# V of group 0 kept on chip, and w_down read in four chunks instead of two

## The chip, the cores and the metric

The kernel runs on one core of one Trainium2 chip. The metric is the device time of one execution in microseconds; less is better. A run is repeated and the median is given.

## The reference

One decode step (one token) of a transformer block, forward and backward, in bf16. With D = 448, 16 query heads, 8 groups of K and V, head size 256, a cache of 32,768 positions of which the last W = 4,096 are attended to, and a gated layer of width F = 1,792:

```python
h  = x + attention(layernorm(x), k_cache, v_cache, wq, wo)   # window: last 4096 positions
h2 = h + (layernorm(h) @ w_gate * (layernorm(h) @ w_up)) @ w_down
# outputs: h2, and the gradients of h2 for grad_out with respect to
# x, k_cache, v_cache, wq, wo, w_gate, w_up, w_down
```

The gradients of the two caches have the caches' full shape, 8 x 32,768 x 256 each. Outside the window they are zero, and these zeros have to be written: 28,672 positions of 256 elements for each group and cache. They are 235 MB of the 281 MB that the kernel writes.

## The kernel before

One large tile, `BIG`, holds nearly all of the on-chip data, by hand-made offsets. It is cut into slots of 8,192 elements a partition (16 KB); a slot takes the window of K or V of one group (partition p holds positions 32p to 32p + 31, as 32 rows of 256). A tile `zeros` has zeros in partitions 32 to 95, the source of the zero fill.

Transfers go out on two queues. SP (`FILL`) reads w_q and then writes zeros in 18 long transfers, one behind the other, over the whole run. GpSimd (`IO`) issues everything else: the loads of K, V and the weights in a fixed order (`io_load` orders each behind the one before it), the computed outputs, and the rest of the zero fill. That rest is dealt by `deal(eng, e0, k, n)`, which writes k x n rows of 16 KB from k source partitions, beginning at partition 32 + 4 e0; `deal_rest(0)` has four such transfers, behind the last load of w_down, and `deal_rest(1)` three, behind the last output.

Forward, for each group in turn (`moments`, `scores`, `softmax`): transposes of K on PE, scores, softmax, and the products of V with p and with p times K. K alternates between two slots (7 and 8). V of groups 0 to 6 was read into `V0` (rows 0 to 24 of group 0, a place of its own), slot 0 (rows 25 to 31 of group 0) and slots 1 to 6; V of group 7 then overwrites slot 0. So all of V but 7 rows of each partition of group 0 is still there for the backward stage.

Then w_o, w_gate and w_up are loaded over the K slots and the space behind them. w_down has 14 rows a partition, in two halves s of 7; one half fits into `wd_sb`. `down_grad(s)` (line 509) forms with DVE the gradient of the hidden values, one instruction of 448 elements for each row, and PE adds the half's share of the output `y` (line 535). The second half is loaded over the first, so its load waits for both. After the second half come the layernorm gradients, the gradients for gate and up (line 563), w_o (line 580) and wq.

Backward through attention, a step for each group in the order `SEQ` (1 to 7, then 0): `dP` transposes V of the next group and multiplies it by the output gradient, beside the 32 matmuls of the step (line 728), whose results go into a pair of slots (`PAIR`), from which two outputs of 2 MB, the window's part of the gradients of K and V, are written (line 737). A pair of slots may be written again when its earlier outputs have landed. `side` lists jobs behind each step: the outer products that form the weights' gradients, in halves of free slots, and the part that reads w_q again for the gradient of x. After step 5 the seven rows of V of group 0 are read once more (line 144), for the last step.

Of the kernel before, what the change touches and what calls it, by code (L numbers as in the profile page):

```python
# [7 lines left out]
bf16 = mybir.dt.bfloat16  # L8
f32 = mybir.dt.float32
# [5 lines left out]
D = 448  # L15
NI = 7
H = 16
G = 8
Dh = 256
W = 4096  # L20
T = 32
F = 1792
FC = 14
Sk = 32768
# [8 lines left out]

KS = 7
TAIL = 9 * SLOT
V0 = TAIL + 8256
NV0 = 25
SIZE = V0 + NV0 * Dh
RING = V0
K_SLOT = [KS + g % 2 for g in range(G)]  # L40
V_SLOT = [0, 1, 2, 3, 4, 5, 6, 0]


@with_exitstack
def kernel(
# [10 lines left out]

    BIG = const.tile([128, SIZE], bf16)
    x_bf = BIG[0:1, TAIL:TAIL + D]
    S_.dma_start(out=x_bf, in_=A_x.rearrange("a b d -> (a b) d"))
    go_bf = BIG[0:1, TAIL + 512:TAIL + 512 + D]  # L60
    S_.dma_start(out=go_bf, in_=grad_out.rearrange("a b d -> (a b) d"))
# [38 lines left out]
    def deal_rest(lap):  # L100
        if lap == 0:
            deal(IO, 0, 4, 25)
            deal(IO, 4, 3, 7)
            deal(IO, 7, 2, 15)
            deal(IO, 9, 7, 15)
        else:
            deal(IO, 0, 5, 2, 512)
            deal(IO, 5, 3, 25)
            deal(IO, 8, 8, 15)
            assert used[0] == 896 * ZW  # L110
# [10 lines left out]
    def slot(k):  # L121
        return BIG[:, k * SLOT:(k + 1) * SLOT]

    def half(k, h):
        return BIG[:, (2 * k + h) * SLOT // 2:(2 * k + h + 1) * SLOT // 2]

    def slot_kv(k):
        return slot(k).rearrange("p (t d) -> p t d", d=Dh)

    Kw = [slot_kv(k) for k in K_SLOT]  # L130
    Vw = [slot_kv(k) for k in V_SLOT]
    v0_head = BIG[:, V0:SIZE].rearrange("p (t d) -> p t d", d=Dh)

# [3 lines left out]
    def v_at(g, t):  # L137
        return v0_head[:, t, :] if g == 0 and t < NV0 else Vw[g][:, t, :]

    queued = [None]  # L140

    def io_load(out, in_):
        if queued[0] is None:
            queued[0] = IO.dma_start(out=out, in_=in_)
        else:
            with tc.issue_after(queued[0].ins):
                queued[0] = IO.dma_start(out=out, in_=in_)

    def load_window(dst, cache, g, n=1):
        src = cache[0, g, Sk - W:, :].rearrange("(p t) d -> p t d", t=T)  # L150
        for h in range(n):
            t = slice(h * T // n, (h + 1) * T // n)
            io_load(dst[:, t, :], src[:, t, :])
# [3 lines left out]

    def load_V(g, head=True):
        if g:
            load_window(Vw[g], A_v_cache, g)  # L160
            return
        src = A_v_cache[0, 0, Sk - W:, :].rearrange("(p t) d -> p t d", t=T)
        if head:
            io_load(v0_head, src[:, 0:NV0, :])
        io_load(Vw[0][:, NV0:T, :], src[:, NV0:T, :])

# [11 lines left out]
    make_identity(nc, ident_f[:])  # L178
    ones_bf = const.tile([1, 128], bf16)
    V_.memset(ones_bf[:], 1.0)  # L180
    ones_f = const.tile([128, 128], f32)
# [146 lines left out]
    def ring(k):  # L328
        return BIG[:, RING - (k + 1) * 1024:RING - k * 1024]

# [101 lines left out]
    WD0 = WG0 + NI * HF  # L432
    assert WD0 + FC // 2 * D == V0

# [11 lines left out]
    wu_sb = BIG[:, WU0:WO1]  # L446
    wd_sb = BIG[:, WD0:V0].rearrange("p (m n) -> p m n", n=D)
    bc2 = [BIG[:, o:o + F].rearrange("p (i c) -> p i c", i=2) for o in (WD0, WD0 - F)]
# [4 lines left out]
    for g in range(G):  # L453
        moments(g)
        if g + 2 < G:
            load_K(g + 2, 2)
        if g + 3 < G:
            load_V(g + 3)
        if g == G - 2:
            load_wo(0, 18)  # L460
        if g == 0:

            t = ps.tile([128, D], f32, tag="tmp", bufs=1)
            P_.matmul(t[:], lhsT=ones_bf[0:1, :], rhs=go_bf, start=True, stop=True)
            S_.copy(out=dh2_bc[:], in_=t[:])
# [31 lines left out]
    io_load(wu_sb, flat_rows(B_w_up))  # L497
    io_load(wd_sb, wd_rows[:, 0])
    hX = const.tile([128, NI], f32)
# [4 lines left out]
    for w, w_sb in ((0, wg_sb), (1, wu_sb)):  # L504
        wv = w_sb.rearrange("p (i c) -> p i c", i=NI)
        for m in range(NI):
            for i in range(NI):
                P_.matmul(gu_ps[:, w, :, m], lhsT=wv[:, i, m::NI], rhs=xx2[:, i, :], start=(i == 0), stop=(i == NI - 1))
    def down_grad(s):
        for m in range(NI):  # L510
            c = NI * s + m
            V_.tensor_tensor_reduce(out=dh_bc[:], in0=wd_sb[:, m, :], in1=dh2_bc[:], scale=1.0, scalar=0.0,
                                    op0=ALU.mult, op1=ALU.add, accum_out=d_hh[:, c:c + 1])

    down_grad(0)
    gu = const.tile([128, 2, FC], f32)
# [9 lines left out]
    V_.tensor_scalar(out=hX2[:], in0=hX[:], scalar1=0.5, scalar2=None, op0=ALU.mult)  # L526
    for s in range(2):
        if s:
            io_load(wd_sb, wd_rows[:, s])
            with tc.issue_after(queued[0].ins):  # L530
                deal_rest(0)
            down_grad(s)
        for m in range(NI):
            c = NI * s + m
            P_.matmul(y[:], lhsT=hh_bf[:, c:c + 1], rhs=wd_sb[:, m, :], start=(c == 0), stop=False, skip_group_check=True)
    half_to_row(y[:], hX2[:], False, first=False)
# [39 lines left out]
    for a in range(4):  # L576
        S_.copy(out=Mq[32 * a:32 * a + 32], in_=quarter(a))
    doW = small.tile([128, 32], f32, tag="doW", bufs=1)
    for b in range(32):
# [5 lines left out]
    V_.tensor_copy(out=doT[:], in_=doT_f[:])  # L585
    od = small.tile([128, 32], f32, tag="od", bufs=1)
    V_.tensor_tensor(out=od[:], in0=doT_f[:], in1=oT_f[:], op=ALU.mult)
# [3 lines left out]
    V_.tensor_copy(out=delta[:], in_=total(pd[:], H)[:])  # L591
    q_rows = BIG[0:H, TAIL:TAIL + Dh]
    do_rows = BIG[0:H, V0 - 320:V0 - 320 + Dh]
    rows16(qT, q_rows, SCALE)
# [3 lines left out]
    for h in range(H):  # L598
        for dk in range(2):
            for hf in range(2):  # L600
# [4 lines left out]
                          start=(hf == 0), stop=(hf == 1))  # L605
    kd = small.tile([128, H, 2], f32, tag="kd", bufs=1)
    V_.tensor_tensor(out=kd[:], in0=kbar[:].rearrange("p (h f) -> p h f", f=2), in1=delta[:].unsqueeze(2).to_broadcast([128, H, 2]), op=ALU.mult)
    dqd = small.tile([128, 32], f32, tag="dqd", bufs=1)
    V_.tensor_tensor(out=dqd[:], in0=dq_ps[:], in1=kd[:].rearrange("p h f -> p (h f)"), op=ALU.subtract)
# [26 lines left out]
    Pq = const.tile([128, NI], f32)  # L636
    wq2 = [slot(4)[:, (i % 4) * HQ:(i % 4 + 1) * HQ] for i in range(NI)]
    wq_d = flat_rows(A_wq).rearrange("p (i c) -> p i c", i=NI)

    def dxn_load(i0, i1):  # L640
        IO.dma_start(out=slot(4)[:, 0:(i1 - i0) * HQ].rearrange("p (i c) -> p i c", c=HQ), in_=wq_d[:, i0:i1, :])

# [5 lines left out]
    def dx_out():  # L648
        dxZ = layernorm_bwd(Pq[:], xh1[:], rstd1[:, 0:1], dhZ[:], 1.0, "dxZ")
        t = ps.tile([1, D], f32, tag="tmp", bufs=1)  # L650
        half_to_row(t[:], dxZ[:], False)
        dx = slot(4)[0:1, SLOT - D:SLOT]
        V_.tensor_copy(out=dx, in_=t[:])
        IO.dma_start(out=out_1.rearrange("a b d -> (a b) d"), in_=dx)
# [4 lines left out]
    def o5_job(buf, b):  # L659
        return lambda: outer(buf, o5[:, b:b + 8, :], b, b + 8, lambda n: dh_bc[:], oW, D)  # L660

    def o67_job(buf, w, i0, i1):
        return lambda: outer(buf, (o6, o7)[w][:, i0:i1, :], i0, i1, lambda i: bc2[w][:, i % 2, :], xf2, HF)

    def o8_job(buf, b):
        return lambda: outer(buf, o8[b // 7], b, b + 7, lambda n: dh2_bc[:], hh, D)

    SEQ = [1, 2, 3, 4, 5, 6, 7, 0]
    PAIR = [KS, 1, KS, 1, KS, 5, 1, KS]
    side = {  # L670
        0: [],
        1: [o67_job(half(3, 0), 0, 0, 4), o67_job(half(3, 1), 0, 4, 7)],
        2: [lambda: dxn_load(0, 4), o5_job(half(3, 0), 0), o5_job(half(3, 1), 8)],
        3: [lambda: dxn_part(0, 4), lambda: dxn_load(4, 7), o5_job(half(3, 0), 16)],
        4: [lambda: dxn_part(4, 7), dx_out, o5_job(half(3, 1), 24), o8_job(half(4, 0), 0)],
        5: [o8_job(half(4, 1), 7), o4_job(half(3, 0), 0), o4_job(half(3, 1), 2)],
        6: [o4_job(half(4, 0), 4), o4_job(half(0, 0), 6)],
        7: [],
    }
    o67_job(half(8, 1), 1, 0, 4)()  # L680
    o67_job(half(7, 1), 1, 4, 7)()


    bps = ctx.enter_context(tc.tile_pool(name="bps", bufs=1, space=bass.MemoryType.PSUM))
    vt_ctr = [0]
    Rb = BIG[:, TAIL + 256:TAIL + 1280].rearrange("p (k c) -> p k c", k=2)
    rows = BIG[:, TAIL + 1280:TAIL + 2304].rearrange("p (a c) -> p a c", a=8)
    VTb = [BIG[:, o:o + 1024] for o in (TAIL + 2304, WD0 + F)]

# [17 lines left out]
    for s, g in enumerate(SEQ):  # L707
# [17 lines left out]
        for t in range(T):  # L725
# [5 lines left out]
            if t % 4 == 3 and s + 1 < G:  # L731
                with tc.issue_after(mm.ins):
                    dP(s + 1, t // 4)
        if s == 5:
            load_V(0, False)
        for w, o in ((0, out_3), (1, out_2)):
# [36 lines left out]
```

## Time and profile before

| | |
|---|---|
| median of 3 runs | 782.29 us (781.71 to 782.57) |
| the profiled execution | 781.56 us; its span 779.8 us |
| moved | 331.13 MB: 49.84 MB read, 280.59 MB written (HBM) |
| mean rate | 425 GB/s |
| busy share of the span | PE 60%, DVE 51%, ACT 24%, POOL 5% |

The profile comes from one execution. "Busy tenths" cut the span into 40 equal slices and give the busy share of each in tenths. DMA is the mean over the core's 16 DMA engines; q1 is SP's queue and q0 is GpSimd's. The packets' own records (start, length, size and queue of each, without the engine's number) are used where a number for one packet is given. The landing time of a transfer goes from its issue to its completion. Line numbers are those of the kernel before.

### The profile page before, as it was taken

The page shows a single profiled execution, that of the slowest core. Times are in us where ns is not written, and L with a number is a line of the kernel's source. Part 1 is how long each engine was busy: PE and PEld are TensorE (multiplying, and loading weights), DVE is VectorE, ACT ScalarE, POOL GpSimd, SP SyncE. Part 2 cuts the span into 40 slices and gives each one's busy share as a digit, 9 for nine tenths or more (in the row PEclk, how much of TensorE's full clock was granted, in tenths as well). Part 3 has the DMA queues.
Part 4 walks back from the last instruction along what each step waited for, and adds up shares of the span by engine and source line. Part 5 has one row for each costly group of instructions (what it writes and reads, how often), then busy time and mean ns, then how long its engine had stood idle before and what let it go on. Part 6 is the DMA issues. An engine that isn't in the chain of part 4 may idle for free.

```text
span 779.8 us, 10845 instructions
## 1 busy us (share of the span) xinstructions
PE 470.1 (60%) x4374; PEld 263.1 (34%) x4419; DVE 401.4 (51%) x1169; ACT 188.7 (24%) x277; POOL 42.0 (5%) x86
## 2 busy tenths in 40 slices
PE   4798898899998642230579879382947696300000
PEld 3654554555564331030254334131423242000000
DVE  5377677677768222659335565367676554300000
ACT  0312322321120000351235435141514353200000
POOL 3000000000000001000000010101001100100000
PEclk9999989989999755555555555555555555555555
DMA  9999999999999999999999999999999999999998
GB/s 351 428 427 428 428 426 430 424 428 429 424 429 427 429 432 429 429 430 429 429 429 430 429 430 429 430 429 430 427 429 432 427 424 431 427 431 430 429 431 344
DMA packets 25234, 331.13 MB, mean 425 GB/s; under 512 B 2669, under 2 KB 2671, under 8 KB 4596
## 3 DMA queue, kind: packets, MB, share of 16 engines
q1 hardware_dynamic: 14557, 231.15, 69.5%
q0 software_dynamic: 10624, 99.29, 30.2%
q8 instruction: 34, 0.56, 0.3%
q14 instruction: 15, 0.12, 0.0%
q10 hardware_dynamic: 4, 0.00, 0.0%
HBM read 49.84 MB, written 280.59 MB: 424 GB/s over the span
## 4 chain that ended last, share of the span: by engine, by line
PE 41%; DMA 18%; DVE 12%; issue 12%; ACT 2%; POOL 1%; POOLq 0%; DVEq 0%; ACTq 0%
PE MT L402 14%; PE d_ps L728 7%; PE tr L345 7%; DMA out_dram<-BIG 6%; DMA BIG<-in_B_w_down_dram 5%; DMA BIG<-in_A_v_cache_dram 4%; DVE BIG L580 2%; PE sT L350 2%; DMA BIG<-in_A_k_cache_dram 2%; PE acc L405 1%; DVE BIG L563 1%; PE acc L408 1%; DMA BIG<-in_A_wq_dram 1%; DVE zeros L419 1%; ACT BIG L293 1%
## 5 line engine op out<-in xcount | busy, mean ns | idle before, releaser
L402 PE MATMUL MT<-BIG 128*128 128x512 bf16 x467 | 139.9, 408 | 1.9 <-DVE BIG L398 0.2
L398 DVE TENSOR_SCALAR BIG<-BIG,pf 128x256 bf16<-128x256 bf16 x512 | 114.3, 281 | 26.6 <-PE MT L402 23.6
L728 PE MATMUL d_ps<-BIG 32*128 32x512 bf16 x256 | 118.9, 620 | 9.1 <-ACT BIG L723 5.4
L345 PE MATMUL tr<-ident_bf,BIG 128*128 128x128 bf16 x1024 | 117.5, 268 | 4.4 <-DMA BIG<-in_A_v_cache_dram 2.9
L295 DVE CAST BIG<-d_ps 128x512 bf16<-128x512 f32 x128 | 88.3, 691 | 56.3 <-PE d_ps L728 55.8
L293 ACT COPY BIG<-tr 128x1024 bf16<-128x1024 bf16 x64 | 64.8, 1012 | 163.3 <-PE tr L345 163.3
L345 PEld LDWEIGHTS <-BIG 128*128 128x128 bf16 x1024 | 78.9, 118 | 43.7 <-issue 40.1
L293 ACT CAST BIG<-d_ps 128x512 bf16<-128x512 f32 x128 | 74.9, 587 | 52.3 <-PE d_ps L728 52.3
L295 DVE COPY BIG<-tr 128x1024 bf16<-128x1024 bf16 x64 | 44.3, 692 | 50.4 <-PE tr L345 48.0
L405 PEld LDWEIGHTS <-BIG 128*128 128x128 bf16 x512 | 42.4, 99 | 53.1 <-issue 17.1
L405 PE MATMUL acc<-pT_all,BIG 128*128 128x2 bf16 x512 | 45.1, 164 | 17.3 <-DVE kbar L424 15.6
L350 PEld LDWEIGHTS <-BIG 128*128 128x128 bf16 x1024 | 39.9, 104 | 40.0 <-DVE BIG L295 20.0
L402 PEld LDWEIGHTS <-BIG 128*128 128x128 bf16 x512 | 40.4, 102 | 23.2 <-issue 16.0
L728 PEld LDWEIGHTS <-BIG 32*128 32x128 bf16 x256 | 27.5, 124 | 56.8 <-issue 56.7
L408 PE MATMUL acc<-pT_all,BIG 128*128 128x2 bf16 x512 | 44.4, 164 | 0.0
L408 PEld LDWEIGHTS <-BIG 128*128 128x128 bf16 x512 | 30.1, 97 | 0.9
L350 PE MATMUL dp<-doT,BIG 128*128 128x2 bf16 x512 | 24.6, 169 | 7.0 <-DVE BIG L295 5.5
L723 ACT CAST BIG<-R_ps 128x512 bf16<-128x512 f32 x8 | 4.7, 586 | 81.4 <-PE R_ps L721 81.4
L350 PE MATMUL sT<-qT,BIG 128*128 128x2 bf16 x512 | 22.5, 165 | 1.1 <-DVE BIG L295 0.8
L715 PE MATMUL r_ps<-ident_bf,pds 128*128 128x128 bf16 x8 | 2.3, 284 | 32.3 <-DVE pds L713 31.6
L645 DVE CUSTOM_DVE_ANT_0 BIG<-BIG,Mt 128x2048 bf16<-128x2048 bf16 x7 | 15.7, 2287 | 7.0 <-DMA BIG<-in_A_wq_dram 7.0
L737 POOL DMA_DIRECT2D out_dram<-BIG x16 | 8.5, 533 | 183.3 <-ACT BIG L293 164.1
(186 smaller groups left out, 375.4 us busy)
## 6 DMA issues: line engine op xcount, KB each, us to landing
out_dram<-zeros SPq DMA_DIRECT2D x15, 14336.0 KB, 152.0
out_dram<-BIG POOLq DMA_DIRECT2D x16, 2048.0 KB, 36.1
BIG<-in_A_v_cache_dram POOLq DMA_DIRECT2D x7, 2048.0 KB, 23.4
BIG<-in_A_k_cache_dram POOLq DMA_DIRECT2D x12, 1024.0 KB, 15.0
out_dram<-zeros SPq DMA_DIRECT2D x1, 6144.0 KB
out_dram<-BIG POOLq DMA_DIRECT2D x6, 896.0 KB, 41.3
BIG<-in_A_k_cache_dram POOLq DMA_DIRECT2D x2, 2048.0 KB, 25.5
out_dram<-BIG POOLq DMA_DIRECT2D x3, 1024.0 KB, 51.7
```

What stands on the lines that cost most here:

```text
L293: S_.copy(out=out, in_=in_)
L295: V_.tensor_copy(out=out, in_=in_)
L345: P_.transpose(tr[:, i, dh, :], x_at(g, 4 * q + i)[:, dh * 128:(dh + 1) * 128], ident_bf[:])
L350: P_.matmul(out_ps[:, 4 * q + i, :], lhsT=xt[:, i, dh, :], rhs=vecT[:, 4 * g + dh:4 * g + dh + 3:2], start=(dh == 0), stop=(dh == 1))
L398: V_.tensor_scalar(out=pk[:, i, h, :], in0=K[:, t, :], scalar1=pf[:, t, h:h + 1], scalar2=None, op0=ALU.mult)
L402: P_.matmul(MT[hf][:], lhsT=v_at(g, t)[:, hf * 128:(hf + 1) * 128], rhs=pk[:, i, :, :].rearrange("p h d -> p (h d)"), start=(t == 0), stop ...
L405: P_.matmul(acc[:, 2 * hf:2 * hf + 2], lhsT=v_at(g, t)[:, hf * 128:(hf + 1) * 128], rhs=pT_all[:, g, t, :], start=(t == 0 and hf == 0), st ...
L408: mm = P_.matmul(acc[:, 4 + dk:7 + dk:2], lhsT=K[:, t, dk * 128:(dk + 1) * 128], rhs=pT_all[:, g, t, :], start=False, stop=(t == T - 1), s ...
L580: V_.tensor_tensor_reduce(out=wg_sb[:, 0:D], in0=parked.get(b, wo_b(b)), in1=dh_bc[:], scale=1.0, scalar=0.0, op0=ALU.mult, op1=ALU.add, a ...
L645: V_.tensor_tensor_reduce(out=wq2[i], in0=wq2[i], in1=dq_bc[:, i % 2, :], scale=1.0, scalar=0.0, op0=ALU.mult, op1=ALU.add, accum_out=Pq[: ...
L728: mm = P_.matmul(d_ps[:].rearrange("p w d -> p (w d)"), lhsT=rows[32 * k:32 * k + 32, a, :], rhs=R[32 * k:32 * k + 32, :], start=True, sto ...
L737: tail = IO.dma_start(out=o[0, g, Sk - W:, :].rearrange("(p t) d -> p t d", t=T), in_=pair[:, w])
```

## The change

V of all groups gets slots of its own (0 to 7), and K moves to slots 8 and 9; `V0` and the second read of group 0's rows are gone. The tile is larger by 448 elements a partition (88,832 for 88,384), and `wd_sb` holds four rows instead of seven. w_down is read in chunks of 4, 3, 4 and 3 rows, each over the one before; `deal_rest(0)` stands behind the fourth. The backward groups go 0 to 7, and the pairs and the slots of the side jobs are other ones. x and grad_out lie in slot 6 at the start. The rows of q (scaled) and of the output gradient, 16 partitions of 2 x 256 elements, lie in partitions 0 to 15 of `zeros`. A few small tiles share buffers. The broadcast of grad_out multiplies in f32, with a copy of grad_out in f32.

```diff
-KS = 7
-TAIL = 9 * SLOT
-V0 = TAIL + 8256
-NV0 = 25
-SIZE = V0 + NV0 * Dh
-RING = V0
+KS = 8
+TAIL = 10 * SLOT
+SIZE = TAIL + 6912
-V_SLOT = [0, 1, 2, 3, 4, 5, 6, 0]
...
-    Vw = [slot_kv(k) for k in V_SLOT]
+    Vw = [slot_kv(g) for g in range(G)]
...
-    def load_V(g, head=True):
-        if g:
-            load_window(Vw[g], A_v_cache, g)
-            return
-        src = A_v_cache[0, 0, Sk - W:, :].rearrange("(p t) d -> p t d", t=T)
-        if head:
-            io_load(v0_head, src[:, 0:NV0, :])
-        io_load(Vw[0][:, NV0:T, :], src[:, NV0:T, :])
+    def load_V(g):
+        load_window(Vw[g], A_v_cache, g)
...
+    CH = ((0, 0, 4), (0, 4, NI), (1, 0, 4), (1, 4, NI))
+    def load_wd(s, m0, m1):
+        io_load(wd_sb[:, 0:m1 - m0, :], wd_rows[:, s].rearrange("j (m n) -> j m n", n=D)[:, m0:m1, :])
...
-            P_.matmul(t[:], lhsT=ones_bf[0:1, :], rhs=go_bf, start=True, stop=True)
+            go_f = BIG[0:1, 6 * SLOT + 1024:6 * SLOT + 1024 + 2 * D].bitcast(f32)
+            V_.tensor_copy(out=go_f, in_=go_bf)
+            P_.matmul(t[:], lhsT=ones_f[0:1, :], rhs=go_f, start=True, stop=True)
...
-    for s in range(2):
-        if s:
-            io_load(wd_sb, wd_rows[:, s])
-            with tc.issue_after(queued[0].ins):
-                deal_rest(0)
-            down_grad(s)
-        for m in range(NI):
+    for n, (s, m0, m1) in enumerate(CH):
+        if n:
+            load_wd(s, m0, m1)
+            if n == len(CH) - 1:
+                with tc.issue_after(queued[0].ins):
+                    deal_rest(0)
+            down_grad(s, m0, m1)
+        for m in range(m0, m1):
             c = NI * s + m
-            P_.matmul(y[:], lhsT=hh_bf[:, c:c + 1], rhs=wd_sb[:, m, :], start=(c == 0), stop=False, skip_group_check=True)
+            P_.matmul(y[:], lhsT=hh_bf[:, c:c + 1], rhs=wd_sb[:, m - m0, :], start=(c == 0), stop=False, skip_group_check=True)
...
-    q_rows = BIG[0:H, TAIL:TAIL + Dh]
-    do_rows = BIG[0:H, V0 - 320:V0 - 320 + Dh]
+    q_rows = zeros[0:H, 0:Dh]
+    do_rows = zeros[0:H, Dh:2 * Dh]
...
-    SEQ = [1, 2, 3, 4, 5, 6, 7, 0]
-    PAIR = [KS, 1, KS, 1, KS, 5, 1, KS]
+    SEQ = list(range(G))
+    PAIR = [KS, 0, KS, 0, KS, 0, 5, KS]
...
-    VTb = [BIG[:, o:o + 1024] for o in (TAIL + 2304, WD0 + F)]
+    VTb = [BIG[:, o:o + 1024] for o in (TAIL + 2048, WD0 - F)]
...
-        if s == 5:
-            load_V(0, False)
```

More of the change, by code (lines that the diff above doesn't have):

```diff
@@ L57 @@
     BIG = const.tile([128, SIZE], bf16)
-    x_bf = BIG[0:1, TAIL:TAIL + D]
+    x_bf = BIG[0:1, 6 * SLOT:6 * SLOT + D]
     S_.dma_start(out=x_bf, in_=A_x.rearrange("a b d -> (a b) d"))
-    go_bf = BIG[0:1, TAIL + 512:TAIL + 512 + D]
+    go_bf = BIG[0:1, 6 * SLOT + 512:6 * SLOT + 512 + D]
     S_.dma_start(out=go_bf, in_=grad_out.rearrange("a b d -> (a b) d"))
@@ L130 @@
     Kw = [slot_kv(k) for k in K_SLOT]
-    Vw = [slot_kv(k) for k in V_SLOT]
-    v0_head = BIG[:, V0:SIZE].rearrange("p (t d) -> p t d", d=Dh)
+    Vw = [slot_kv(g) for g in range(G)]
     def k_at(g, t):
@@ L137, in v_at @@
     def v_at(g, t):
-        return v0_head[:, t, :] if g == 0 and t < NV0 else Vw[g][:, t, :]
+        return Vw[g][:, t, :]
     queued = [None]
@@ L178 @@
     make_identity(nc, ident_f[:])
-    ones_bf = const.tile([1, 128], bf16)
-    V_.memset(ones_bf[:], 1.0)
     ones_f = const.tile([128, 128], f32)
@@ L328, in ring @@
     def ring(k):
-        return BIG[:, RING - (k + 1) * 1024:RING - k * 1024]
+        return BIG[:, SIZE - (k + 1) * 1024:SIZE - k * 1024]
     def kt_buf():
@@ L432 @@
     WD0 = WG0 + NI * HF
-    assert WD0 + FC // 2 * D == V0
+    CH = ((0, 0, 4), (0, 4, NI), (1, 0, 4), (1, 4, NI))
+    assert WD0 + 4 * D == SIZE
     def wo_at(b):
@@ L446 @@
     wu_sb = BIG[:, WU0:WO1]
-    wd_sb = BIG[:, WD0:V0].rearrange("p (m n) -> p m n", n=D)
+    wd_sb = BIG[:, WD0:SIZE].rearrange("p (m n) -> p m n", n=D)
+    def load_wd(s, m0, m1):
+        io_load(wd_sb[:, 0:m1 - m0, :], wd_rows[:, s].rearrange("j (m n) -> j m n", n=D)[:, m0:m1, :])
     bc2 = [BIG[:, o:o + F].rearrange("p (i c) -> p i c", i=2) for o in (WD0, WD0 - F)]
@@ L497 @@
     io_load(wu_sb, flat_rows(B_w_up))
-    io_load(wd_sb, wd_rows[:, 0])
+    load_wd(*CH[0])
     hX = const.tile([128, NI], f32)
@@ L508, with down_grad @@
                 P_.matmul(gu_ps[:, w, :, m], lhsT=wv[:, i, m::NI], rhs=xx2[:, i, :], start=(i == 0), stop=(i == NI - 1))
-    def down_grad(s):
-        for m in range(NI):
+    def down_grad(s, m0, m1):
+        for m in range(m0, m1):
             c = NI * s + m
-            V_.tensor_tensor_reduce(out=dh_bc[:], in0=wd_sb[:, m, :], in1=dh2_bc[:], scale=1.0, scalar=0.0,
+            V_.tensor_tensor_reduce(out=dh_bc[:], in0=wd_sb[:, m - m0, :], in1=dh2_bc[:], scale=1.0, scalar=0.0,
                                     op0=ALU.mult, op1=ALU.add, accum_out=d_hh[:, c:c + 1])
-    down_grad(0)
+    down_grad(*CH[0])
     gu = const.tile([128, 2, FC], f32)
@@ L526 @@
     V_.tensor_scalar(out=hX2[:], in0=hX[:], scalar1=0.5, scalar2=None, op0=ALU.mult)
-    for s in range(2):
-        if s:
-            io_load(wd_sb, wd_rows[:, s])
-            with tc.issue_after(queued[0].ins):
-                deal_rest(0)
-            down_grad(s)
-        for m in range(NI):
+    for n, (s, m0, m1) in enumerate(CH):
[5 more added lines that the diff above has]
+            down_grad(s, m0, m1)
+        for m in range(m0, m1):
             c = NI * s + m
-            P_.matmul(y[:], lhsT=hh_bf[:, c:c + 1], rhs=wd_sb[:, m, :], start=(c == 0), stop=False, skip_group_check=True)
+            P_.matmul(y[:], lhsT=hh_bf[:, c:c + 1], rhs=wd_sb[:, m - m0, :], start=(c == 0), stop=False, skip_group_check=True)
     half_to_row(y[:], hX2[:], False, first=False)
@@ L577 @@
         S_.copy(out=Mq[32 * a:32 * a + 32], in_=quarter(a))
-    doW = small.tile([128, 32], f32, tag="doW", bufs=1)
+    doW = small.tile([128, 32], f32, tag="ef", bufs=1)
     for b in range(32):
@@ L585 @@
     V_.tensor_copy(out=doT[:], in_=doT_f[:])
-    od = small.tile([128, 32], f32, tag="od", bufs=1)
+    od = small.tile([128, 32], f32, tag="ex", bufs=1)
     V_.tensor_tensor(out=od[:], in0=doT_f[:], in1=oT_f[:], op=ALU.mult)
@@ L605 @@
                           start=(hf == 0), stop=(hf == 1))
-    kd = small.tile([128, H, 2], f32, tag="kd", bufs=1)
+    kd = small.tile([128, H, 2], f32, tag="pp", bufs=2)
     V_.tensor_tensor(out=kd[:], in0=kbar[:].rearrange("p (h f) -> p h f", f=2), in1=delta[:].unsqueeze(2).to_broadcast([128, H, 2]), op=ALU.mult)
-    dqd = small.tile([128, 32], f32, tag="dqd", bufs=1)
+    dqd = small.tile([128, 32], f32, tag="pp", bufs=2)
     V_.tensor_tensor(out=dqd[:], in0=dq_ps[:], in1=kd[:].rearrange("p h f -> p (h f)"), op=ALU.subtract)
@@ L636 @@
     Pq = const.tile([128, NI], f32)
-    wq2 = [slot(4)[:, (i % 4) * HQ:(i % 4 + 1) * HQ] for i in range(NI)]
+    wq2 = [slot(3)[:, (i % 4) * HQ:(i % 4 + 1) * HQ] for i in range(NI)]
     wq_d = flat_rows(A_wq).rearrange("p (i c) -> p i c", i=NI)
     def dxn_load(i0, i1):
-        IO.dma_start(out=slot(4)[:, 0:(i1 - i0) * HQ].rearrange("p (i c) -> p i c", c=HQ), in_=wq_d[:, i0:i1, :])
+        IO.dma_start(out=slot(3)[:, 0:(i1 - i0) * HQ].rearrange("p (i c) -> p i c", c=HQ), in_=wq_d[:, i0:i1, :])
     def dxn_part(i0, i1):
@@ L651, in dx_out @@
         half_to_row(t[:], dxZ[:], False)
-        dx = slot(4)[0:1, SLOT - D:SLOT]
+        dx = slot(3)[0:1, SLOT - D:SLOT]
         V_.tensor_copy(out=dx, in_=t[:])
@@ L666, in o8_job @@
         return lambda: outer(buf, o8[b // 7], b, b + 7, lambda n: dh2_bc[:], hh, D)
-    SEQ = [1, 2, 3, 4, 5, 6, 7, 0]
-    PAIR = [KS, 1, KS, 1, KS, 5, 1, KS]
+    SEQ = list(range(G))
+    PAIR = [KS, 0, KS, 0, KS, 0, 5, KS]
     side = {
         0: [],
[L672 to L677, printed above, removed]
+        1: [o67_job(half(2, 0), 0, 0, 4), o67_job(half(2, 1), 0, 4, 7)],
+        2: [lambda: dxn_load(0, 4), o5_job(half(2, 0), 0), o5_job(half(2, 1), 8)],
+        3: [lambda: dxn_part(0, 4), lambda: dxn_load(4, 7), o5_job(half(4, 0), 16)],
+        4: [lambda: dxn_part(4, 7), dx_out, o5_job(half(4, 1), 24), o8_job(half(2, 0), 0)],
+        5: [o8_job(half(2, 1), 7), o4_job(half(4, 0), 0), o4_job(half(4, 1), 2)],
+        6: [o4_job(half(3, 0), 4), o4_job(half(3, 1), 6)],
         7: [],
     }
-    o67_job(half(8, 1), 1, 0, 4)()
-    o67_job(half(7, 1), 1, 4, 7)()
+    o67_job(half(KS + 1, 1), 1, 0, 4)()
+    o67_job(half(KS, 1), 1, 4, 7)()
     bps = ctx.enter_context(tc.tile_pool(name="bps", bufs=1, space=bass.MemoryType.PSUM))
     vt_ctr = [0]
-    Rb = BIG[:, TAIL + 256:TAIL + 1280].rearrange("p (k c) -> p k c", k=2)
-    rows = BIG[:, TAIL + 1280:TAIL + 2304].rearrange("p (a c) -> p a c", a=8)
-    VTb = [BIG[:, o:o + 1024] for o in (TAIL + 2304, WD0 + F)]
+    Rb = BIG[:, TAIL:TAIL + 1024].rearrange("p (k c) -> p k c", k=2)
+    rows = BIG[:, TAIL + 1024:TAIL + 2048].rearrange("p (a c) -> p a c", a=8)
+    VTb = [BIG[:, o:o + 1024] for o in (TAIL + 2048, WD0 - F)]
     def vt_buf():
```

## The prediction, made before the changed kernel ran

> **What bounds the kernel now.** I read the page's slices first, because they show at once whether compute or transfers set the time. PE is busy in the first two thirds and then falls to zero; the DMA row never leaves 9 until the last slice.
>
> ```profile
> span 779.8 us, 10845 instructions
> ...
> PE   4798898899998642230579879382947696300000
> ...
> DMA  9999999999999999999999999999999999999998
> ...
> q1 hardware_dynamic: 14557, 231.15, 69.5%
> q0 software_dynamic: 10624, 99.29, 30.2%
> ```
>
> To be seen: all 16 DMA engines work from the first microseconds to the last, 70% of their time for SP's queue (the zero fill) and 30% for GpSimd's queue (the loads and the computed outputs). PE has nothing left in the last five slices. Next, the stages, to see what happens once compute is over (columns: stretch, its length, busy time of each engine, granted PE clock, DMA share, GB/s):
>
> ```profile
> 400.00:675.00 275.00, 195.57 (x1217) 88.55 (x1214) 158.89 (x284) 105.01 (x164) 18.41 (x34) 0.50 1.01 429
> 675.00:700.00 25.00, 0.00 (x0) 0.00 (x0) 0.00 (x0) 0.00 (x0) 0.63 (x1) 0.50 1.01 430
> ...
> 770.00:772.00 2.00, 0.00 (x0) 0.00 (x0) 0.00 (x0) 0.00 (x0) 0.00 (x0) 0.50 0.98 417
> 772.00:774.00 2.00, 0.00 (x0) 0.00 (x0) 0.00 (x0) 0.00 (x0) 0.00 (x0) 0.50 0.84 360
> 774.00:776.00 2.00, 0.00 (x0) 0.00 (x0) 0.00 (x0) 0.00 (x0) 0.00 (x0) 0.50 0.83 349
> 776.00:780.00 4.00, 0.00 (x0) 0.00 (x0) 0.00 (x0) 0.00 (x0) 0.00 (x0) 0.50 0.18 72
> ```
>
> No compute engine runs after 675 us, and the rate is the same 429 to 430 GB/s with and without compute beside it. Only after 770 does the share drop: the engines come to their ends one by one (the packet records put the ends of the last small zero packets between 769.7 and 778.4). So the time is the work dealt to the DMA engine that ends last. A wait on PE, DVE or ACT costs nothing while both queues have something for every engine. The page's chain, 41% PE, is misleading here: it follows instructions, and the fill needs none after it has been issued.
>
> Third, GpSimd's queue at its end, and the two transfers that the change touches:
>
> ```profile
> 293.82 0.53 POOL L147 DMA_DIRECT2D BIG<-in_B_w_down_dram  x1 [34.37 <-DVE d_hh L512]
> ```
>
> ```profile
> 615.06 0.55 POOL L144 DMA_DIRECT2D BIG<-in_A_v_cache_dram  x1 [23.71 <-PE tr L345]
> ...
> 670.79 1.06 POOL L737 DMA_DIRECT2D out_dram<-BIG  x2 [19.25 <-issue]
> 671.84 1.28 POOL L77 DMA_DIRECT2D out_dram<-zeros  x2
> 675.49 0.63 POOL L77 DMA_DIRECT2D out_dram<-zeros  x1 [2.37 <-DMA out_dram<-BIG]
> ```
>
> The last transfer is issued at 675.5, about 100 us before the end. Line 144 is the second read of rows 25 to 31 of V of group 0.
>
> **The change, part by part.**
>
> *V of group 0 stays.* The second read goes: 448 KB, 0.459 MB. At 429 GB/s that is 1.07 us of all 16 engines. From the packets themselves: 64 packets of 7,168 bytes near 640 us, 280 ns each, 17.9 us in all, over 16 engines 1.12 us. Of the 64, 58 start within 4.1 us; four turns of one such packet and one 16 KB zero packet (611 ns) take 3.6 us, so four packets for each engine fit, and every engine, the last one too, is relieved alike. I take 1.1 us. The first read comes as one load of 2,048 KB instead of 1,600 and 448: the same bytes, nothing.
>
> *w_down in four chunks.* The bytes stay. Rows of 6,272 bytes were recorded in pairs, 128 packets of 12,544 at 469 ns (60.0 us); rows of 3,584 pair to 7,168 (64 a load, two loads, 272 ns: 34.8 us) and rows of 2,688, if they pair, to 5,376, a size that the outputs have at 206 ns (26.4 us): 61.2 us, 0.07 us more for each engine. Unpaired, going along the line through those sizes (about 6 ns a packet besides the bytes), 0.2 us. I take 0.1 us. The number of GpSimd's transfers stays (two fewer for V, two more here), so the completion packets do as well.
>
> In the compute chain this is the large part. Before, the second half is issued at 293.8, lands after 11.8 us, takes 4.6 us of `down_grad`, and all is done at 310.3. After it, three loads follow each other, since each overwrites the buffer that the one before has filled: chunk 0 (read by about 287.5, hh is ready at 284.9), 2.7 us of gradients, then three times some 11 us to land and 0.6 to issue, with 2.0, 2.7 and 2.0 us of gradients: done at about 331, 21 us later. Behind the waiting loads on GpSimd stand the four zero fills of `deal_rest(0)`, then everything of the backward stage. Its cover is the fill on SP: at 676 us the engines have, on average, 73 us of q1 packets and 28 us of q0 packets left, by the records. If that cover were gone, the 21 us would show in full.
>
> *Backward groups 0 to 7.* In the old step for group 7, PE waits 2.9 us for the rows reread; gone. The old sixth step writes into slots 5 and 6 without waiting for an output; now it writes into slots 0 and 1, which the fourth step's outputs leave. Those were issued at 530.4 and landed after 28.6 us (559), while the sixth step begins to write about 590; all move by the same 21 us, so there is no wait even if they land as slowly as the last ones (46.9 us, to 577). The seventh step now takes slots 5 and 6, whose V is used up, instead of waiting for those outputs. The side jobs use other slots but keep their order on GpSimd. I put 0 to +10 us on this, within the chain only.
>
> *Small things.* q and do rows beside the zeros: the same two ACT copies, into partitions 0 to 15, which no zero fill reads (it reads partitions 32 to 92). One f32 matmul 128x448 for a bf16 one, one DVE copy more, one memset fewer: under 2 us of the chain, long before the end. Shared buffers for doW, od, kd, dqd: the earlier users are done by then. The second buffer of `vt_buf` now lies where GpSimd's last w_up outer product reads from, which DVE has finished by 373 us, before the first write near 390.
>
> So the last issue moves from 675.5 to about 690 to 705. From which point would that count? If the last issue is d later, SP's packets fill the gap until they are used up: d of 73 us on average, some 8 less on the three engines to which lap 1 deals 25 packets (15.3 us against a mean of 7.4). That is a last issue near 740, and 705 leaves 35 us.
>
> Sum for the profiled execution: its own time is 781.56 (the span of 779.8 and 1.8 around it); minus 1.1, plus 0.1, gives 780.6. The median of the runs shown is 782.29, 0.7 above that execution, so the median should come to about 781.3, 0.13% less. What a measurement of this kernel can tell from no change is about 0.2%, 1.6 us; the forecast lies inside that.
>
> [...] The stretch from 400 to 675 us has 429 GB/s with reads and writes mixed, and that is the rate used above. [...]
>
> **The rivals.**
>
> *The relief is uneven.* The end is one engine's, and the records do not name engines. If the 64 packets went to eight engines only, eight each, the last engine gains either 2.2 us (780.1 to 780.2 for the median) or nothing (782.3, with the smaller chunks 782.4). For it: the ends spread over 8.7 us, so engines do carry different loads. Against: eight turns would take 7.1 us, and 58 of 64 starts lie in 4.1 us.
>
> *The zero fills land on other engines: slower.* `deal` gives unequal numbers of 16 KB packets to small sets of engines. Taking engine numbers as the arguments have them, lap 0 and lap 1 together give 25 packets to engines 0 to 3, 7 to engine 4, 32 to 5 and 6, 40 to 7, and 30 to the rest. The ends within 8.7 us say that this offsets loads elsewhere. If the engines were chosen by what GpSimd has issued so far, one more transfer ahead of lap 0 (a V load fewer, two w_down loads more) would turn the pattern by one: engine 4 gets 25 instead of 7, 18 packets of 0.611 us, 11.0 us later. As its own end is 0 to 8.7 us before the last, the end moves by 2.3 to 11, less 1.0: 783.6 to 792.3. It decides as soon as the pattern turns at all. Against: the four sets of lap 0 (4, 3, 2, 7) sum to 16, as do those of lap 1 (5, 3, 8), so a position moved on by the size of each set comes round to where it was, and a transfer over all 16 would not move it. [...]
>
> *The chain becomes the end.* If w_down's loads queue as V's reread did (31.6 us to land) and the backward steps add waits of that size at several pairs, the last issue passes the point worked out above (740 to 748), and each further microsecond counts in full. Three loads at 31.6 instead of 11 are +62, with the 21 it is 83: last issue at 758, 10 to 18 too late, time 792 to 800. Against: all w_down loads go out while GpSimd's queue is empty, as the 11.8 us one did.
>
> *The bytes were free:* 782.3. Against: there is no idle DMA stretch after the first microseconds in which they could have hidden.
>
> **How the numbers follow.** Even relief has 0.64, with 780.5 to 782.1 as its own range (the runs shown differ by 0.9 in all); 0.12 of it I put below the 0.2% bound, since the price per engine and the scatter are each uncertain by a few tenths. The gaining half of uneven relief has 0.11; its losing half and the free bytes, which read alike, 0.12; turned fills 0.07; the chain 0.06. Faster by over 0.2%: 0.12 + 0.11 = 0.23; within: 0.52 + 0.12 = 0.64; slower: 0.13. The range reaches down to the uneven gain, 779.9, and up past no gain, 782.6; the two slow cases stay out.
>
> **What would show it.** HBM reads fall from 49.84 to 49.38 MB; line 144's late read is missing; w_down shows 448 and 336 KB loads landing in 10 to 13 us, and three waits of PE for them instead of one long one; the last GpSimd issue falls at 690 to 705; the DMA row is 9 up to the last slice; the share drops after about 769, with ends spread as before. Wrong if the DMA row shows a gap before 760, if the ends spread over clearly more or less than 8.7 us, or if the time moves by more than 1.6 us with the same spread.

## The result, and the profile after

The changed kernel takes 788.58 us (median of 6 runs, 786.81 to 789.22) against 782.29 (781.33 to 783.64) for the kernel before, a ratio of 1.0077 [1.0063, 1.0091]. It is slower by 6.3 us, where 781.3 and a range of 779.9 to 782.6 had been forecast. The profiled execution took 786.81 us, the fastest of the six; the profiled one of before took 781.56. Its page, in the lines that answer to those of before:

```profile
span 784.9 us, 10845 instructions
...
PE   4798898899998631313258897639392889700000
...
DMA  9999999999999999999999999999999999999997
...
q1 hardware_dynamic: 14557, 231.15, 69.4%
q0 software_dynamic: 10496, 98.83, 30.0%
...
HBM read 49.38 MB, written 280.59 MB: 420 GB/s over the span
```

The DMA row is 9 in every slice but the last, so the end is still set by the transfers. The bytes fell as forecast: the kernel before read 49.84 MB and moved 99.29 MB on q0. Fewer bytes took longer. The stages show where (columns: stretch, its length, busy time of PE, PE weight loads, DVE, ACT and POOL, granted PE clock, DMA share, GB/s):

```profile
400.00:675.00 275.00, 198.13 (x1321) 94.89 (x1322) 155.03 (x278) 104.08 (x160) 15.86 (x29) 0.50 1.01 424
675.00:700.00 25.00, 8.15 (x21) 2.21 (x19) 7.65 (x12) 6.02 (x11) 2.95 (x5) 0.50 1.01 422
700.00:740.00 40.00, 0.00 (x0) 0.00 (x0) 0.00 (x0) 0.00 (x0) 0.00 (x0) 0.50 1.01 427
...
770.00:772.00 2.00, 0.00 (x0) 0.00 (x0) 0.00 (x0) 0.00 (x0) 0.00 (x0) 0.50 0.96 410
772.00:780.00 8.00, 0.00 (x0) 0.00 (x0) 0.00 (x0) 0.00 (x0) 0.00 (x0) 0.50 0.77 325
```

The rate from 400 to 675 us is 424 GB/s where it was 429; the engines are as full as before and move less. From 700 to 740 us, when no engine computes in either kernel, it is 427 where the kernel before has 430:

```profile
700.00:740.00 40.00, 0.00 (x0) 0.00 (x0) 0.00 (x0) 0.00 (x0) 0.00 (x0) 0.50 1.01 430
```

Last, GpSimd's queue: the three w_down loads that overwrite the chunk before, and its end.

```profile
290.66 0.54 POOL L142 DMA_DIRECT2D BIG<-in_B_w_down_dram  x1 [29.56 <-PE y L530]
301.66 0.54 POOL L142 DMA_DIRECT2D BIG<-in_B_w_down_dram  x1 [10.45 <-DVE d_hh L506]
313.04 0.54 POOL L142 DMA_DIRECT2D BIG<-in_B_w_down_dram  x1 [10.85 <-DVE d_hh L506]
...
690.55 0.63 POOL L73 DMA_DIRECT2D out_dram<-zeros  x1 [3.30 <-DMA out_dram<-BIG]
```

The loads follow each other by 11.0 and 11.4 us. Each landed 8.3 to 8.7 us after its issue, sooner than the 10 to 13 us forecast. The last issue moved from 675.49 to 690.55, inside the forecast 690 to 705, at its early end.

The packets' own records say what became slow. A 16 KB zero packet of SP's queue took 611 ns before, with few exceptions: from 400 to 770 us a share of 0.05 took over 612 ns, and the mean was 612.9. In the changed kernel the share is 0.46 and the mean 621.0. From 100 to 300 us both kernels have 0.06, with means of 614.1 and 613.6. The slow packets come in stretches: about 388 to 515 us, 575 to 585, and 615 to the end. Each of the first two ends in a burst of longer packets, in the time of a w_q load: the first load was issued at 503.5 us and landed 23.2 us later, and the second one's 128 packets, of 12,288 bytes, start between 579.9 and 592.3. The stages show the first burst:

```profile
510.00:515.00 5.00, 0.00 (x0) 0.00 (x0) 0.00 (x0) 0.00 (x0) 0.53 (x1) 0.50 1.00 354
515.00:520.00 5.00, 0.66 (x2) 0.20 (x2) 3.42 (x11) 0.00 (x0) 0.53 (x1) 0.50 1.03 436
```

354 GB/s at a full DMA share, then 436 in the next 5 us. In sum, the packets of the changed kernel keep an engine busy for 783.1 us on average, before 780.0. That is 3.1 more although the bytes removed are worth 1.0, so some 4.1 us are longer packets. (The records of 16 KB packets alone, after 385 us: 5.2 us beyond 611 ns for each engine, 1.3 before; the difference is 3.9.) The two profiled executions differ by 5.25 us, and the rest of that is imbalance. The records do not name engines; strung into 16 rows, in which each packet begins where another ended, they give the engines' ends. The mean of the 16 ends moved from 776.1 to 779.2 and the last of them from 778.4 to 783.5, so the slow packets fell unevenly and the last engine stands 4.3 instead of 2.3 us above the mean. That makes 5.1 us. In the second execution below (again, 788.83 us) they are 779.7 and 785.5.

### The profile page after: what moved, and what is told of

It is laid out like the page before. It is cut to its first block, busy times and chain, and to the rows that moved or that the text cites. A ratio compares the mean times of both kernels' runs of the same rounds, so it can differ in the third digit from the quotient of the medians.

```text
span 784.9 us, 10845 instructions
## 1 busy us (share of the span) xinstructions
PE 472.8 (60%) x4375; PEld 263.8 (34%) x4420; DVE 401.5 (51%) x1169; ACT 188.5 (24%) x277; POOL 42.3 (5%) x86
## 4 chain that ended last, share of the span: by engine, by line
PE 46%; DMA 17%; DVE 15%; issue 7%; ACT 2%; POOL 1%; POOLq 0%; DVEq 0%; ACTq 0%
PE MT L389 14%; PE d_ps L723 10%; PE tr L332 9%; DMA BIG<-in_B_w_down_dram 7%; DMA out_dram<-BIG 6%; DMA BIG<-in_A_wq_dram 3%; DVE BIG L575 2%; PE sT L337 2%; DMA BIG<-in_A_k_cache_dram 2%; DVE BIG L558 1%; PE acc L392 1%; PE acc L395 1%; DVE zeros L406 1%; PE dp L337 1%; DVE BIG L282 1%
## 5 line engine op out<-in xcount | busy, mean ns | idle before, releaser
L389 PE MATMUL MT<-BIG 128*128 128x512 bf16 x467 | 141.7, 412 | 2.0 <-DVE BIG L385 0.2
L506 DVE CUSTOM_DVE_ANT_0 dh_bc<-BIG,dh_bc 128x448 bf16<-128x448 bf16 x14 | 8.7, 625 | 39.5 <-DMA BIG<-in_B_w_down_dram 39.3
L530 PE MATMUL y<-BIG,hh_bf 128*1 128x448 bf16 x14 | 5.9, 566 | 31.5 <-DMA BIG<-in_B_w_down_dram 28.1
```

What stands on the lines that cost most here:

```text
L389: P_.matmul(MT[hf][:], lhsT=v_at(g, t)[:, hf * 128:(hf + 1) * 128], rhs=pk[:, i, :, :].rearrange("p h d -> p (h d)"), start=(t == 0), stop ...
L506: V_.tensor_tensor_reduce(out=dh_bc[:], in0=wd_sb[:, m - m0, :], in1=dh2_bc[:], scale=1.0, scalar=0.0, op0=ALU.mult, op1=ALU.add, accum_ou ...
```

## The experiments

The theories, with the letters that the expectations give them. **Rows (R):** the rows of q and of the output gradient lie in the zero tile, and writing or reading them disturbs the fill. **Order (O):** the new backward order and slots do. **Turned fills:** as in the prediction. **Later (T):** the backward stage comes 15 us later and meets the fill otherwise. N is something outside the kernel. **Place (A):** `BIG` is 896 bytes a partition larger, so `zeros`, which is allocated behind it, begins at byte 194,176 of the partition instead of 193,280. The old start is a multiple of 256, the new one is 128 off.

All measured times (us), with the ratio to the kernel before measured beside it, the share of SP's 16 KB zero packets over 612 ns from 400 to 770 us, and the mean and last of the engines' ends. Shares and ends come from the one profiled execution of each run; those of after (786.81 us), b_chunks (784.28) and a_gap5 (784.39) lie off their medians. "off" is the start of `zeros` modulo 256.

| run | off | median | ratio [95%] | share | ends |
|---|---|---|---|---|---|
| before | 0 | 782.29 | 1 | 0.05 | 776.1, 778.4 |
| after | 128 | 788.58 | 1.0077 [1.0063, 1.0091] | 0.46 | 779.2, 783.5 |
| again (one run) | 128 | 788.83 | beside 781.92 | 0.47 | 779.7, 785.5 |
| b_rows | 0 | 782.24 | 1.0002 [0.9993, 1.0011] | 0.06 | 776.2, 779.1 |
| a_apart | 128 | 788.04 | 1.0072 [1.0055, 1.0088] | 0.45 | 779.5, 785.0 |
| b_chunks | 0 | 783.07 | 1.0016 [1.0007, 1.0025] | 0.06 | 776.4, 779.7 |
| a_order | 128 | 789.42 | 1.0087 [1.0067, 1.0107] | 0.46 | 779.6, 786.2 |
| b_noreload | 0 | 780.46 | 0.9978 [0.9969, 0.9987] | 0.06 | 775.1, 777.3 |
| a_gap | 0 | 780.45 | 0.9981 [0.9970, 0.9992] | 0.07 | 774.8, 777.3 |
| b_gap | 128 | 787.72 | 1.0071 [1.0056, 1.0086] | 0.39 | 780.3, 784.5 |
| b_gap64 | 64 | 787.79 | 1.0080 [1.0065, 1.0095] | 0.39 | 780.5, 784.5 |
| b_gap192 | 192 | 787.65 | 1.0076 [1.0059, 1.0093] | 0.40 | 780.5, 784.4 |
| b_gap256 | 0 | 781.92 | 1.0005 [0.9996, 1.0015] | 0.06 | 776.3, 778.7 |
| b_gap_late | 128 | 790.39 | 1.0112 [1.0097, 1.0127] | 0.34 | other end, see below |
| after_load | 128 | 790.69 | 1.0112 [1.0095, 1.0130] | 0.38 | 780.8, 787.2 |
| a_gap5 | 0 | 780.40 | 0.9985 [0.9977, 0.9994] | 0.07 | 775.0, 781.2 |
| gap_first | 0 | 779.19 | 0.9966 [0.9954, 0.9979] | 0.04 | 774.3, 775.9 |

**again:** the changed kernel once more.

> The changed kernel once more, for its trace. In its first profile the 16 KB zero packets take 611 ns until about 388 us, then 615 to 622 ns on a third to three quarters of them (388 to 514 us and from 615 us to the end). Theory R (the q and output-gradient rows, written into partitions 0 to 15 of the zeros at 388 us, slow the fill that reads the same tile): the same onset within 2 us, the same share from then on. Theory T (the backward stage stands 15 us later against the fill, so that outputs and fill meet in memory at other places): the same stretches again, since the order is the same. Theory N (something outside the kernel): no such stretch, or stretches at other times, and a time near 781.

788.83 us, with the same stretches; the first begins at about 360 instead of 388 us. So the slow packets are no accident of one execution.

**b_rows and a_apart:** the rows put into the zeros of the kernel before, and taken out of them in the changed one.

```diff
-    q_rows = BIG[0:H, TAIL:TAIL + Dh]
-    do_rows = BIG[0:H, V0 - 320:V0 - 320 + Dh]
+    q_rows = zeros[0:H, 0:Dh]
+    do_rows = zeros[0:H, Dh:2 * Dh]
```

```diff
-    q_rows = zeros[0:H, 0:Dh]
-    do_rows = zeros[0:H, Dh:2 * Dh]
+    q_rows = BIG[0:H, TAIL + 3072:TAIL + 3072 + Dh]
+    do_rows = BIG[0:H, TAIL + 4352:TAIL + 4352 + Dh]
...
-    rows16(doT, do_rows, 1.0)
...
+    rows16(doT, do_rows, 1.0)
```

> The kernel before, with the q and output-gradient rows in partitions 0 to 15 of the zeros and nothing else. Theory R: slow packets from about 373 us on (where these rows are written there), 4 us more for the mean engine, time 786 to 789. Theories T and N and the turned fills: no change, 781.5 to 783.

> The changed kernel, with the q and output-gradient rows in free places of the big tile (the second written behind the two early outer products) and not beside the zeros. Theory R: 16 KB zero packets back to 611 ns throughout, 781 to 782. Theory T, turned fills: 787 to 789 as the changed kernel.

Neither moved the time. The rows beside the zeros are out.

**b_chunks:** w_down's four chunks alone, in the kernel before.

```diff
-    io_load(wd_sb, wd_rows[:, 0])
+    load_wd(*CH[0])
...
-    for s in range(2):
-        if s:
-            io_load(wd_sb, wd_rows[:, s])
+    for n, (s, m0, m1) in enumerate(CH):
+        if n:
+            load_wd(s, m0, m1)
...
```

> The kernel before, with w_down read in the four chunks of 4, 3, 4, 3 rows and nothing else: the backward stage and the first dealt fills come some 20 us later, two more loads stand ahead of the first dealt fills. Theory T: most of the loss, 785 to 789, with slow packets in similar stretches. Turned fills: 784 to 800 with 611 ns packets and ends spread over far more than 9 us. Theory R: no change, 782 to 783 (0.1 for the smaller packets).

Two more loads stand ahead of the fills of lap 0, and the ends stay between 770.5 and 779.7 us: no engine is 11 us later, so the fills did not turn here. The backward stage is as late as in the changed kernel (PE runs up to the stretch 675 to 700, the last issues lie there), and the slow packets do not come (0.06); the rate stays at 429:

```profile
400.00:675.00 275.00, 197.78 (x1320) 94.81 (x1320) 154.98 (x278) 103.63 (x159) 16.02 (x30) 0.51 1.01 429
675.00:700.00 25.00, 8.50 (x22) 2.27 (x20) 8.00 (x12) 6.24 (x11) 2.95 (x5) 0.50 1.01 429
```

That takes away "turned fills" and "later" as the cause. The median is 1.2 us above the kernel before, though (783.07 beside 781.92; 0.16%, 0.07 to 0.25). It stands between two groups: five executions took 781.95 to 782.52 us and five 783.61 to 784.53.

**a_order:** the changed kernel with the old order of the groups, pairs and side slots.

```diff
-    SEQ = list(range(G))
-    PAIR = [KS, 0, KS, 0, KS, 0, 5, KS]
+    SEQ = [1, 2, 3, 4, 5, 6, 7, 0]
+    PAIR = [KS, 1, KS, 1, KS, 5, 1, KS]
...
```

> The changed kernel with the backward groups in the old order 1 to 7, 0, and the pairs and side jobs in the slots that they had. Theory O: back to 781 to 782.5. Theories A and T: 787 to 789.

789.42, as slow as the changed kernel: the order is out.

**a_gap and b_gap:** an unused tile of 128 bytes a partition between `BIG` and `zeros`. It puts the zeros of the changed kernel on a multiple of 256 (194,304) and those of the kernel before off one (193,408). The small tiles that are allocated behind the zeros move with them, and there is one small DVE instruction more; all else stays.

```diff
+    gap = const.tile([128, 64], bf16)
...
+    V_.memset(gap[0:1, 0:2], 0.0)
```

> The changed kernel with 128 unused bytes a partition between the big tile and the zeros. As the big tile is 896 bytes larger than before, the zeros begin 128 bytes behind a multiple of 256 in the changed kernel (194,176), and on a multiple of 256 in the kernel before (193,280); the gap puts them on 194,304, a multiple again. Theory A (the place of the zeros: each 16 KB packet that starts off a 256-byte boundary takes up to a few more ns): zero packets at 611 ns throughout, time 781 to 782.5. Theory T (meeting of outputs and fill) or O (order of the groups): 787 to 789 as before.

> The kernel before with the same gap of 128 bytes: here it puts the zeros 128 bytes behind a multiple of 256. Theory A: the slow zero packets of 615 to 622 ns appear in the kernel before, 786 to 790. Theories T and O: no change, 781.5 to 783.

The same edit makes the one faster by 8.1 us (788.58 to 780.45; 7.5 by the ratios) and the other slower by 5.6 (787.72 beside 782.09). The stages of b_gap and then of a_gap:

```profile
400.00:675.00 275.00, 195.71 (x1218) 88.68 (x1215) 158.94 (x284) 105.08 (x164) 16.82 (x32) 0.50 1.01 424
675.00:700.00 25.00, 0.00 (x0) 0.00 (x0) 0.00 (x0) 0.00 (x0) 2.16 (x4) 0.50 1.01 424
700.00:740.00 40.00, 0.00 (x0) 0.00 (x0) 0.00 (x0) 0.00 (x0) 0.00 (x0) 0.50 1.01 426
```

```profile
400.00:675.00 275.00, 202.95 (x1332) 96.21 (x1331) 159.24 (x284) 107.22 (x165) 15.85 (x29) 0.50 1.01 429
675.00:700.00 25.00, 3.17 (x9) 0.79 (x6) 3.46 (x5) 2.48 (x5) 2.95 (x5) 0.50 1.01 427
700.00:740.00 40.00, 0.00 (x0) 0.00 (x0) 0.00 (x0) 0.00 (x0) 0.00 (x0) 0.50 1.01 430
```

424 GB/s came to the old kernel and left the new one, with the place of the zeros and of the small tiles behind them. Of these only the zeros are read by a transfer, and the packets stay slow from 700 us on, when no engine computes. So the place of the zeros is the cause of the loss. a_gap came out a little below its 781 to 782.5, and faster than the kernel before by 1.6 us (by the interval 0.6 to 2.3).

**b_gap64, b_gap192, b_gap256:** is it any distance from the multiple of 256, does it grow with the distance, or does the gap itself cost? The gap has 32, 96 and 128 elements.

> The kernel before with a gap of 64 bytes: the zeros begin 64 behind a multiple of 256. Theory A in the form that each packet moves the extra bytes up to the next boundary: half of the extra of 128, slow packets near 613 to 616 ns, time 784 to 786. In the form that only being off the boundary counts: as with 128, 787 to 789.

> The kernel before with a gap of 192 bytes: the zeros begin 192 behind a multiple of 256. Theory A with extra bytes: half as much again as 128, slow packets 618 to 625 ns, 789 to 792. With being off the boundary alone: 787 to 789.

> The kernel before with a gap of 256 bytes: the zeros move, but stay on a multiple of 256 (193,536). Theory A (the remainder by 256 decides): no change, 781.5 to 783, zero packets 611 ns. If any move of the tile were to blame: 786 to 790.

64, 128 and 192 bytes off cost the same, +0.7 to +0.8%, and 256 costs nothing (1.0005 [0.9996, 1.0015]). So in these runs the price does not depend on the distance. Nor is it there from the start: for the first 360 us the packets off the multiple take 611 ns like those on it (from 100 to 300 us the share over 612 is 0.06 in the changed kernel as in the one before).

**b_noreload:** what the bytes are worth by themselves.

```diff
-        if s == 5:
-            load_V(0, False)
```

> The kernel before without the second read of V of group 0; it leaves this read out, and the last step takes group 7's rows in their place. The price of the bytes alone: 780.7 to 781.5, 1.1 below the kernel before, if every engine is relieved alike; under 0.3 if the end is set by an engine that had no part in it.

780.46, which is 1.6 us less than 782.09 beside it (by the interval 1.0 to 2.4). That is just below the 780.7 to 781.5 expected, and 1.1 lies in the interval: the reload's price holds. The relief looks even: the mean of the ends moved from 776.1 to 775.1, the last from 778.4 to 777.3.

**b_gap_late:** in b_gap the first stretch begins at about 385 us, after the four unequal fills of lap 0 (issued at 294.6); here they go out at the end instead, ahead of lap 1's.

```diff
-            with tc.issue_after(queued[0].ins):
-                deal_rest(0)
...
+        deal_rest(0)
```

> The kernel before with the gap of 128 bytes, and with the four unequal fills of deal_rest(0) moved from behind w_down to the end, ahead of deal_rest(1). If the slow packets need engines that have been moved apart by these unequal fills (in the runs with 128 bytes they begin some 5 to 50 us after them): zero packets stay at 611 ns from 390 to 490 us, and most of the loss is gone, 782 to 785. If off-boundary packets are slow by themselves once the long loads are over: slow from about 390 us as before, 787 to 789.

The first stretch begins at about 430 us instead of 385, but the stretches come, so the unequal fills aren't needed for them. The gain that was hoped for is missing (790.39). The zeros' last packets, here on GpSimd's queue, end at 784.2, as in b_gap (784.5), but the span ends at 788.4. These 4.2 us behind the last packet, where most runs have 1.4, make the time longer than b_gap's; they say nothing on the stretches.

**after_load:** the first stretch of b_gap ends near 500 us, in the time of a w_q load, and its stretch from 615 ends near 642 to 647, where V's reload moves (its packets start between 642.2 and 648.8). So one load of 448 KB was put into the changed kernel, behind the last output, and ahead of lap 1's fills. It reads V rows into a slot whose data is used up.

```diff
     with tc.issue_after(tail.ins):
+        tail = IO.dma_start(out=Vw[7][:, 25:T, :], in_=A_v_cache[0, 0, Sk - W:, :].rearrange("(p t) d -> p t d", t=T)[:, 25:T, :])
+    with tc.issue_after(tail.ins):
         deal_rest(1)
```

> The changed kernel with one load more, of 448 KB, into rows that nobody reads any more, issued behind the last output (near 686 us) and ahead of the last dealt fills. If a load ends a slow stretch: zero packets are slow until the load's packets run (about 710 to 735 us, the outputs stand ahead of it), and at 611 ns for the 30 us and more behind it. If a stretch ends by itself: the share above 612 ns stays at 0.6 to 0.8 until 770. Time 787 to 790 either way, as the load takes 1.1 us itself.

```profile
686.90 0.55 POOL L734 DMA_DIRECT2D BIG<-in_A_v_cache_dram  x1
```

It is issued at 686.9, but its 64 packets start only between 735.1 and 743.3. From 680 to 720 us the share over 612 ns is 0.67 to 0.70, from 720 to 740 it is 0.57, and from 741 on it is 0.00, every packet at 611.0 ns up to the end (in the changed kernel 0.76 from 740 to 760). In this trace a load ends a stretch. It comes too late to pay for itself: 790.69, above the 787 to 790 expected.

**a_gap5 and gap_first:** in all kernels so far `BIG` itself begins at 16,512, 128 off a multiple of 256, and is the source of the outputs. In gap_first the 128-byte tile stands ahead of `BIG`, so that both begin on a multiple (16,640 and 194,304); a_gap5 is a_gap once more, run beside it.

```diff
+    gap = const.tile([128, 64], bf16)
     BIG = const.tile([128, SIZE], bf16)
...
```

> The changed kernel with the gap of 128 bytes between the big tile and the zeros, once more, beside the other gap and in more rounds: 780.3 to 780.7, 0.2% below the kernel before.

> The changed kernel with the 128 unused bytes ahead of the big tile instead of behind it: now both the big tile (16,640) and the zeros (194,304) begin on a multiple of 256. If outputs whose source lies off a boundary are slow too: up to 0.5 us below the gap in the other place, 779.8 to 780.5. If not: the same as it, 780.3 to 780.7.

779.19 against 780.40, and the best of all: 0.9966 [0.9954, 0.9979] of the kernel before. It lies below the 779.8 to 780.5 expected, and its slowest execution (779.66) is faster than a_gap5's fastest (780.04).

```profile
400.00:675.00 275.00, 202.66 (x1333) 96.33 (x1333) 158.78 (x284) 106.70 (x164) 15.87 (x29) 0.50 1.01 430
675.00:700.00 25.00, 3.68 (x10) 0.86 (x8) 3.88 (x6) 2.83 (x5) 2.95 (x5) 0.50 1.01 431
700.00:740.00 40.00, 0.00 (x0) 0.00 (x0) 0.00 (x0) 0.00 (x0) 0.00 (x0) 0.50 1.01 431
```

431 GB/s from 675 to 740 us, where a_gap has 427 and 430. After 680 us one of SP's 1,702 packets of 16 KB is over 612 ns, in a_gap 102 of 1,705; the engines end at 774.3 on average, the last at 775.9. `BIG` is the source of the outputs and the target of the loads; which of the two gains was not tried apart.

## Why the prediction was wrong

*What bounds the kernel* was right: transfers, to the last slice, before and after. No compute wait entered the end.

*V of group 0 stays* was right in size: 1.1 us forecast, 1.6 (1.0 to 2.4) in b_noreload, 0.9 in the packets' sum per engine (780.0 to 779.1).

*w_down in four chunks* was right in the chain's form, and too long in its size. The loads follow each other, and PE waits for them three times, 28.1 us in all,

```profile
PE y L530 <- DMA BIG<-in_B_w_down_dram: 28.1, 3, 10.1
```

but they land in 8.3 to 8.7 us where some 11 were taken, so the last issue comes 15 us later and not 21, far from the 740 at which it would count. The term in the sum was too small: 0.1 us forecast, 1.2 (0.5 to 2.0) in b_chunks. The packets' sum has 0.3 of it (780.3 for 780.0). The profiled execution (784.28, of the slower group) has a span 2.7 us longer than the kernel before; of this 1.0 more lies between the mean and the last end, and 1.4 more behind the last packet (779.7 to 782.5, before 778.4 to 779.8). What divides the two groups is open. It does not simply add to the other terms, since a_gap, which has the chunks and lacks the reload, gained 1.6 us, as much as b_noreload without the chunks.

*Backward groups 0 to 7* was right: a_order gained nothing.

*Small things* is the step that failed. That the tile is larger by 448 elements had been noted under the change, but the prediction has no term for it: this step put the zeros at nothing because no fill reads the rows beside them, and the sum took a zero packet to cost what it did before. I looked at what is read and not at where it begins. Those 896 bytes move the source of 70% of the DMA time by three times 256 and 128 bytes, and that costs 7.5 to 8.1 us of the 788.58 (a_gap against the changed kernel). Without it the forecast sum stands, within the range: 780.45 and 780.40 measured, 781.3 forecast; and the packets' sum of a_gap is 1.1 us less for each engine than before (778.9 for 780.0), where 1.0 had been forecast.

*The rivals.* "The zero fills land on other engines" named 783.6 to 792.3, and the result lies in there by luck, for another reason: in b_chunks nothing turned, nor in a_gap, which has all transfers of the changed kernel and ends between 768.7 and 777.3 us. "The chain becomes the end" is refuted by the last issue at 690.55, "the bytes were free" by b_noreload, and its ends, the mean and the last both about 1 us earlier, speak against "the relief is uneven". None had a price on where the source begins.

*What would show it.* The test in the text worked: the ends spread over 10.4 us (773.1 to 783.5) where the kernel before, read in the same way, has 7.9, and the time moved by more than 1.6. The slowdown itself was to be seen in the rate of the stages, 424 for 429, which the prediction did not list.

## What to carry to other kernels

When a kernel is bound by its DMA engines, a change of a tile's size also moves the tiles allocated behind it (here 896 bytes moved `zeros` from 193,280 to 194,176); work out where the sources of the large transfers begin, modulo 256 bytes, before and after: here 64, 128 and 192 bytes off cost 0.7 to 0.8% (b_gap64, b_gap, b_gap192), and a gap of 256 cost nothing (b_gap256). When a DMA-bound kernel with fewer bytes is slower, compare GB/s and the time of one packet in stages whose DMA share is full: from 400 to 675 us both kernels have a share of 1.01, and one moves 429 GB/s, the other 424. A one-line gap tile, put into both kernels, told the placement effect from all that the change does (788.58 to 780.45 us in the one, 787.72 beside 782.09 in the other).

## What the hardware showed that was not expected

With `zeros` off a multiple of 256 bytes, these kernels' fill was not slower always, but in stretches: the same 16 KB packets take 611 ns up to about 360 to 430 us (again, after, b_gap, b_gap_late), then in the long stretches a share of about 0.3 to 0.8 of them takes over 612 (typically 613 to 625). In after_load a stretch ended with the packets of the load put in, which run from 735 us on: a share of 0.57 before them, 0.00 from 741 us. That is shown in this one trace. The ends near 515 and 585 us of the changed kernel, and those near 500, 570 and 645 us of b_gap, fall together with loads as well, and the changed kernel, which has no reload at 640, stays slow from 615 to the end (a share of 0.76 from 740 to 760 us). Up to 300 us, where K, V and weights are loaded one after the other, no stretch came (0.06 from 100 to 300 us); that the loads keep them away was not shown, and what begins a stretch stays open. The bursts, such as 354 GB/s at a full share before 515 us, are seen and not explained.
